# Linear attention and a SiLU feed-forward layer on one core: batch 1's exp(k), the PSUM banks of two chunks, a weight sum and the last store rearranged

## The chip, the core and the metric

The kernel runs on one NeuronCore of a Trainium2 chip. A core has a matrix engine (TensorE, PE, with its own path for loading weights, PEld), three engines for elementwise work (VectorE, DVE; ScalarE, ACT; GpSimd, POOL), a queue engine (SyncE, SP), and sixteen DMA engines that all the queues share. They run side by side and wait for each other by semaphores. TensorE writes its results to PSUM, here one tile of 8 banks of 512 float32 columns on 128 partitions. The metric is the device time of one execution in microseconds.

## What is computed

```python
def _attn_ref(q, k, v) -> np.ndarray:      # 8 batches, 8 heads, 576 rows, 64 columns
    q_s = q - np.max(q, axis=-1, keepdims=True)
    q_s = np.exp(q_s)
    q_s = q_s / (np.sum(q_s, axis=-1, keepdims=True) + 1e-09)
    k_s = k - np.max(k, axis=2, keepdims=True)
    k_s = np.exp(k_s)
    k_s = k_s / (np.sum(k_s, axis=2, keepdims=True) + 1e-09)
    kv = np.einsum('bhsd,bhse->bhde', k_s, v)
    return np.einsum('bhsd,bhde->bhse', q_s, kv).astype(np.float32)
...
def _moe_ref(x, w_in, w_out) -> np.ndarray:   # 4608 x 512, 512 x 2048, 2048 x 512
    h = x @ w_in
    g = h * (1.0 / (1.0 + np.exp(-h)))
    return (g @ w_out).astype(np.float32)
```

The attention's output, its heads side by side, is the `x` of the second function.

## The kernel before

**Batches and chunks.** A batch has 576 token rows. The feed-forward layer works on chunks of 512 token columns, nine in all, so that chunk 1 needs the end of batch 0 and most of batch 1. For each batch, ACT takes exp(q) and exp(k) (`exp_q` L105, `exp_k` L110), q is normalized on DVE or POOL (`qnorm` L152), v is cast into `vaug` (`vcast` L113), PE multiplies k and v (`kv` L183), DVE divides the result into `kvn` (`kvcopy` L195), and PE makes x from the transposed q and `kvn` (`xt` L236). Loads of q, k and v go through two buffers for each name and half, so a load of batch 2 waits until batch 1's reader of the same buffer has run.

**First stage.** Chunk 0 is computed with batch 0 whole (576 columns): sixteen `wide` units (L606) of the first product, each into two PSUM banks, followed by a tanh on ACT (L248) and one DVE pass (L249) that writes `GT`. Chunk 0's second product, `mm2_plain` (L394), accumulates into banks 2 to 5 over sixteen units. Chunk 1's first product, `mm1` (L288), is interleaved with its last six units; its sixteen products use the banks of the table `A1_BANKS` (L271), and each is followed by a tanh on ACT and a pass on DVE. When `mm2_plain` is done, `mm2_plain_out` (L404) takes two of its banks out, one by ACT (L408) and one by DVE (L410).

**Later chunks.** From chunk 2 on, both products use a Strassen-Winograd scheme with seven block products in place of eight. `group` (L345) is the first product: it uses banks 0 to 3, its adds are at L337 and its activations at L343. `prod` (L444) is the second product: by default it uses banks 4 and 5, with snapshots to SBUF by ACT (L474). Sums of weights that the scheme needs are made once: `ws_op` (L304) for the first weight matrix, `t_op` (L434) for the second; its second sum, T2 = B22 - T1, is made on DVE in two halves (L442), and its third and fourth on POOL. Sums of the data blocks are made by `s_op` (L423). The second product of the last chunk stands alone at the end and is written out in `end` (L725): the chain of products 1, 6 and 7 accumulates in bank 3, product 4 is in bank 1, 2 in bank 5, and 5 and 3 in banks 4 and 0. `part` (L703) makes a quarter of the output with one DVE instruction and stores it in two pieces, on the queues given there.

**Order.** The order is written out by hand. The work is a list of units; `plan(u, f)` (L603) puts a function ahead of unit u, in the order of the calls, and the loop at L801 runs all of it. Each engine executes its own instructions in that order. `b1` is 16, the first unit behind the wide stage. Unit b1 + 9 is the last `mm2_plain` unit without an interleaved `mm1`; from b1 + 10 to b1 + 21, `mm1` products 0 to 5 stand at even offsets and `mm2_plain` units at odd ones; `mm1` product 6 is unit b1 + 22, and so on to b1 + 31.

Of the kernel before, what the change touches and what calls it, by code (L numbers as in the profile page):

```python
# [17 lines left out]
def kernel(  # L18
# [9 lines left out]
    nc = tc.nc  # L28
# [64 lines left out]
    def load(b, name, src, cc, eng):  # L93
        t = ld.tile([128, 2, J * D], FP32, name=name)
        st[b][name, cc] = t
        x = src[b].rearrange("(g r) (p j) d -> g (r p) (j d)", r=2, j=J)
        eng.dma_start(out=t, in_=x.rearrange("g x y -> x g y")[:, 2 * cc:2 * cc + 2, :])  # L97

    def jgd(b, name, cc):
        return st[b][name, cc].rearrange("p g (j d) -> p j g d", d=D)  # L100

    def half(t, cc):
        return t[:, :, cc * 128:(cc + 1) * 128].rearrange("p j (g d) -> p j g d", d=D)

    def exp_q(b, cc):  # L105
        if "eq" not in st[b]:
            st[b]["eq"] = ap.tile([128, J, NG * D], BF16, name="eq")
        nc.scalar.activation(out=half(st[b]["eq"], cc), in_=jgd(b, "qt", cc), func=ACT.Exp)  # L108

    def exp_k(b, cc):  # L110
        nc.scalar.activation(out=half(ek, cc), in_=jgd(b, "kt", cc), func=ACT.Exp)  # L111
# [6 lines left out]
    def qsum_pair(b, cc):  # L118
        e = half(st[b]["eq"], cc)
        t1 = mp.tile([128, 2 * TCH], FP32, name="h0", bufs=1)[:, 0:J * D]  # L120
        t1 = t1.rearrange("p (j g d) -> p j g d", g=2, d=D // 2)
        t2 = mp.tile([128, 2 * TCH], FP32, name=f"h{cc + 1}", bufs=1)[:, 0:J * D // 2]
        t2 = t2.rearrange("p (j g d) -> p j g d", g=2, d=D // 4)
        nc.gpsimd.tensor_tensor(  # L124
            out=t1, in0=e[:, :, :, 0:D // 2], in1=e[:, :, :, D // 2:D], op=ALU.add
        )
        nc.gpsimd.tensor_tensor(
            out=t2, in0=t1[:, :, :, 0:D // 4], in1=t1[:, :, :, D // 4:D // 2], op=ALU.add
        )
        st[b]["t2", cc] = t2  # L130

    def qsum_end(b, cc):
        new_zq(b)
        nc.vector.reduce_sum(out=st[b]["zq"][:, cc], in_=st[b]["t2", cc], axis=AX.X)
        nc.vector.reciprocal(out=st[b]["rzq"][:, cc], in_=st[b]["zq"][:, cc])
# [16 lines left out]
    def qnorm(b, cc, eng):  # L152
        e = half(st[b]["eq"], cc)
        r = st[b]["rzq"][:, cc]
        eng.tensor_tensor(  # L155
            out=e, in0=e, in1=r[:, :, :, None].to_broadcast([128, J, 2, D]), op=ALU.mult
        )
# [110 lines left out]
            GTS[0][:, fb, :].rearrange("p (a n) -> p a n", a=2), S,  # L268
        )

    A1_BANKS = [0, 1, 0, 1, 0, 1, 2, 0, 3, 1, 0, 2, 1, 0, 2, 3]  # L271

    def mm1_mm(t, fb, bank, cs):
        o0 = pieces(t)[0][3]
        for c in cs:
            nc.tensor.matmul(  # L276
                out=PS[:, bank, o0:TCH],
                lhsT=W1[:, c, fb * 128:(fb + 1) * 128],
                rhs=XTS[t % 2][:, c, o0:TCH],
                start=(c == 0),  # L280
                stop=(c == NC - 1),
            )

    def mm1_silu(t, fb, bank):
        o0 = pieces(t)[0][3]
        silu(t, fb, PS[:, bank, o0:TCH], GTS[t % 2][:, fb, o0:TCH], TCH - o0)

    def mm1(t, i):  # L288
        mm1_mm(t, FB[i], A1_BANKS[i], range(NC))
        mm1_silu(t, FB[i], A1_BANKS[i])  # L290

# [94 lines left out]
    def rows(t, col):  # L386
        b, c = divmod(t * TCH + col, S)
        return out[b * S:(b + 1) * S, :].rearrange("(p j) o -> j p o", j=J)[c // P]
# [31 lines left out]
    def blk(t, kh, th):  # L420
        return GTS[t % 2][:, kh * HF:(kh + 1) * HF, th * HT:(th + 1) * HT]
# [12 lines left out]
    def t_op(i, eng, f0=0, f1=HF):  # L434
        o, in0, in1 = {
            1: (T1, B12, B11),
            2: (T2, B22, T1),
            3: (T3, B22, B12),
            4: (T4, B21, T2),
        }[i]  # L440
        f = slice(f0, f1)
        eng.tensor_tensor(out=o[:, f], in0=in0[:, f], in1=in1[:, f], op=ALU.subtract)  # L442

    def prod(t, i, m, bank=None, fresh=None, done=None):  # L444
        bank = WBANK[i] if bank is None else bank
        a, bb = {
            1: (blk(t, 0, 0), B11),
            2: (blk(t, 1, 0), B21),
            3: (SS[4], B22),
            4: (blk(t, 1, 1), T4),  # L450
            5: (SS[1], T1),
            6: (SS[2], T2),
            7: (blk(t, 0, 1), T3),
        }[i]
        first = (m == 0 and i in (1, 2, 5)) if fresh is None else fresh
        done = (m == 1 and i in (4, 3, 2)) if done is None else done
        for fc in range(HF):
            nc.tensor.matmul(  # L458
                out=PS[:, bank, m * HN:(m + 1) * HN],
                lhsT=a[:, fc, m * 128:(m + 1) * 128],  # L460
                rhs=bb[:, fc, :],
                start=(first and fc == 0),
                stop=(done and fc == HF - 1),
                skip_group_check=True,
            )

    def w_out_tile(t, m):
        if ("o", m) not in WG[t]:
            WG[t]["o", m] = mp.tile([128, 2, DM], FP32, name="ow", bufs=3)
        return WG[t]["o", m]  # L470

    def snap(t, name, bank=4):
        WG[t][name] = mp.tile([128, 512], FP32, name=name, bufs=1)
        nc.scalar.activation(out=WG[t][name], in_=PS[:, bank, :], func=ACT.Copy, scale=OS)  # L474
# [65 lines left out]
    def load_w2(f0, f1):  # L540
        nc.gpsimd.dma_start(
            out=W2[:, f0:f1, :],
            in_=w_out[f0 * 128:f1 * 128, :].rearrange("(fc p) o -> p fc o", p=128),
        )
# [58 lines left out]
    def plan(u, f):  # L603
        at.setdefault(u, []).append(f)
# [92 lines left out]
    last = NCH - 1  # L697
# [5 lines left out]
    def part(name, bank, th, n, a):  # L703
        o = w_out_tile(last, th)[:, a, n * HN:(n + 1) * HN]
        nc.vector.scalar_tensor_tensor(  # L705
            out=o,
            in0=PS[:, bank, a * HN:(a + 1) * HN],
            scalar=OS,
            in1=WG[last][name][:, a * HN:(a + 1) * HN],
            op0=ALU.mult,  # L710
            op1=ALU.add,
        )
        one, two = {
            (0, 0): (nc.sync, nc.sync),
            (1, 1): (nc.gpsimd, nc.gpsimd),
            (1, 0): (nc.scalar, nc.sync),
            (0, 1): (nc.scalar, nc.gpsimd) if a == 0 else (nc.sync, nc.sync),
        }[th, n]
        for i, eng in enumerate((one, two)):
            eng.dma_start(  # L720
                out=rows(last, th * HT + a * 128 + i * P)[:, n * HN:(n + 1) * HN],
                in_=o[i * P:(i + 1) * P, :],
            )

    def end(i, m):  # L725
        if i in (5, 3):
            prod(last, i, m, bank=(4, 0)[m], fresh=(i == 5), done=(i == 3))
        elif i == 4:
            prod(last, i, m, bank=1, fresh=(m == 0), done=(m == 1))
        else:  # L730
            prod(last, i, m, bank=5 if i == 2 else 3)
        if i == 3:
            part("sb", (4, 0)[m], 0, 1, m)
        elif m == 1 and i in (1, 6, 7):
            snap(last, {1: "sa", 6: "sb", 7: "sc"}[i], 3)
        if m == 1 and i == 2:
            part("sa", 5, 0, 0, 0)
            part("sa", 5, 0, 0, 1)
        elif m == 1 and i == 7:
            part("sc", 4, 1, 1, 0)  # L740
            part("sc", 0, 1, 1, 1)
        elif m == 1 and i == 4:
            part("sc", 1, 1, 0, 0)
            part("sc", 1, 1, 0, 1)

    for i in (1, 2, 6, 5, 7, 4, 3):
        for m in range(2):
# [3 lines left out]
    b1 = begin[1]  # L751
# [6 lines left out]
    plan(9, lambda: (load_w2(8, 12), exp_q(1, 0), qsum_pair(1, 0)))  # L758
    plan(10, lambda: (load(2, "qt", q, 0, nc.gpsimd), load(2, "qt", q, 1, nc.gpsimd)))
    plan(11, lambda: (exp_q(1, 1), qsum_end(1, 0), qnorm(1, 0, nc.gpsimd), qsum_pair(1, 1)))  # L760
    plan(13, lambda: exp_k(1, 0))
    plan(15, lambda: exp_k(1, 1))
    plan(b1, lambda: (tr(1, 0, 0, 5, 6), tr(1, 0, 5, J, 7)))
    plan(b1, lambda: (trcopy(1, 0, 0, 5, 6, nc.scalar), trcopy(1, 0, 5, J, 7)))
    plan(b1, lambda: (qsum_end(1, 1), qnorm(1, 1, nc.vector)))
    plan(b1, lambda: load_w2(12, 16))
    plan(b1, lambda: (load(2, "kt", k, 0, nc.gpsimd), load(2, "kt", k, 1, nc.gpsimd)))
    plan(b1, lambda: nc.gpsimd.tensor_copy(GTS[1][:, :, 0:64], GTS[0][:, :, TCH:S]))
    plan(b1 + 6, lambda: (load(2, "vt", v, 0, nc.gpsimd), load(2, "vt", v, 1, nc.gpsimd)))
    plan(b1 + 4, lambda: vcast(1, 0, nc.scalar))  # L770
    plan(b1 + 5, lambda: (tr(1, 1, 0, 5, 0), tr(1, 1, 5, J, 1)))
# [14 lines left out]
    plan(b1 + 14, lambda: q_transpose(2))  # L786
    for i, x in enumerate((16, 18)):
        plan(b1 + x, lambda i=i: (exp_k(2, i), vcast(2, i, nc.gpsimd)))
    plan(b1 + 18, lambda: t_op(2, nc.vector, 0, 4))
    plan(b1 + 20, lambda: t_op(2, nc.vector, 4, 8))  # L790
    plan(b1 + 20, lambda: loads(3, nc.sync))
    plan(b1 + 22, lambda: mm2_plain_out(0, (0, 1)))
    plan(b1 + 23, lambda: kv_both(2))
# [42 lines left out]
```

## Time and profile before

Device time over seven runs, and the one execution that was profiled:

| | us |
|---|---|
| median of 7 runs | 265.92 |
| lowest and highest | 264.84 to 266.93 |
| profiled execution, its time | 264.83 |
| its span, first to last instruction | 263.0 |
| from the span to the time, around it | 1.83 |
| PE busy | 254.8 |
| DVE busy | 209.7 |
| ACT busy | 182.6 |
| POOL busy | 74.7 |

The busy times are those of the profiled execution and overlap each other. A line of a timeline has the start in us, the length in us, the engine, the line of the kernel, the operation, what it writes and reads with partitions x elements, and how many instructions are merged in it; in brackets stands the idle time before it with what ended the wait. PE products are pipelined, so that the end of one is shown later than the start of the next. A line of a table by stage has the stretch, its length, then for PE, PEld, DVE, ACT and POOL the busy us with the number of instructions, and at the end the granted TensorE clock (1.00 is full), the mean share of the DMA engines in use, and GB/s.

### The profile page before, as it was taken

How to read it: one execution, taken by the hardware profiler on the slowest of the kernel's cores; microseconds unless marked ns; L12 is line 12 of the kernel's file. 1: busy time of each engine (PE TensorE's matmuls, PEld its weight loads, DVE VectorE, ACT ScalarE, POOL GpSimd, SP SyncE). 2: the span in 40 equal slices, each digit the busy share in tenths (PEclk: the TensorE clock that was granted, in tenths of full speed). 3: DMA queues.
4: the chain of work that ended last, by engine and by line, in shares of the span. 5: the costliest groups of instructions: out<-in, count | busy, mean ns of one | idle time of the engine just before them, and what ended most of it. 6: DMA issues, size and time to landing. Idle time of an engine off the chain costs nothing.

```text
span 263.0 us, 6375 instructions
## 1 busy us (share of the span) xinstructions
PE 254.8 (97%) x2708; PEld 201.4 (77%) x2708; DVE 209.7 (80%) x276; ACT 182.6 (69%) x209; POOL 74.7 (28%) x65
## 2 busy tenths in 40 slices
PE   8999999999999999999999999999999999999993
PEld 2467644445888888888888888888888888888782
DVE  2867789987997999799979997999798548855832
ACT  5767955748796699669966996699664747484610
POOL 1743981697360306030603060306000000000004
PEclk9999999999999999999999999999999999999999
DMA  7999999689978487957784878440415004300634
GB/s 244 331 200 330 259 324 333 242 168 384 331 267 195 130 210 260 171 154 193 275 199 129 209 260 206 121 107 2 90 36 126 2 0 92 70 2 1 134 68 120
DMA packets 35452, 45.89 MB, mean 174 GB/s; under 512 B 16208, under 2 KB 19984, under 8 KB 35424
## 3 DMA queue, kind: packets, MB, share of 16 engines
q1 hardware_dynamic: 29568, 33.69, 46.4%
q0 software_dynamic: 5616, 11.60, 16.8%
q8 instruction: 21, 0.34, 0.5%
q10 hardware_dynamic: 240, 0.20, 0.3%
q14 instruction: 7, 0.06, 0.1%
HBM read 36.70 MB, written 9.44 MB: 175 GB/s over the span
## 4 chain that ended last, share of the span: by engine, by line
PE 84%; DVE 6%; DMA 4%; ACT 2%; POOL 2%; SPq 1%; issue 1%; POOLq 0%; DVEq 0%; ACTq 0%
PE PS L458 36%; PE PS L359 33%; PE PS L256 4%; PE PS L276 4%; DMA vt<-in_v_dram 4%; PE PS L396 3%; PE PS L187 2%; PE PS L226 2%; DVE WS L312 1%; DVE GT L249 1%; DVE zq L148 1%; SPq L97 1%; POOL out_dram L720 1%; POOL h L124 0%; DVE h L337 0%
## 5 line engine op out<-in xcount | busy, mean ns | idle before, releaser
L337 DVE TENSOR_TENSOR h<-PS,h 128x1024 f32<-128x1024 f32 x42 | 50.7, 1207 | 11.2 <-PE PS L359 5.8
L458 PEld LDWEIGHTS <-GT 128*128 128x128 f16 x512 | 49.6, 98 | 7.4 <-issue 1.6
L458 PE MATMUL PS<-W,GT 128*128 128x256 f16 x384 | 49.1, 273 | 0.4 <-DVE h L337 0.4
L359 PEld LDWEIGHTS <-WS 128*128 128x128 f16 x448 | 43.7, 98 | 5.7 <-issue 0.6
L155 POOL TENSOR_TENSOR eq<-eq,rzq 128x1152 bf16<-128x1152 bf16 x13 | 27.5, 2117 | 60.3 <-DVE rzq L150 56.2
L359 PE MATMUL PS<-XS,WS 128*128 128x256 f16 x336 | 43.5, 273 | 0.0
L343 ACT ACTIVATE GT<-h 128x1024 f16<-128x1024 f32 x42 | 43.3, 1054 | 0.3 <-DVE h L337 0.3
L89 ACT COPY h<-PS 128x1024 f32<-128x1024 f32 x32 | 32.4, 1012 | 13.7 <-PE PS L359 13.3
L458 PEld LDWEIGHTS <-S 128*128 128x128 f16 x384 | 37.2, 98 | 5.2 <-issue 1.0
L359 PEld LDWEIGHTS <-W 128*128 128x128 f16 x336 | 32.5, 98 | 4.4 <-issue 0.2
L458 PE MATMUL PS<-T,S 128*128 128x256 f16 x256 | 32.7, 273 | 0.0
L359 PE MATMUL PS<-XT,W 128*128 128x256 f16 x224 | 27.9, 273 | 0.0
L249 DVE SCALAR_TENSOR_TENSOR GT<-sg,PS 128x576 f16<-128x576 f32 (+1 forms) x32 | 21.2, 680 | 8.2 <-ACT sg L248 8.0
L343 ACT ACTIVATE GT<-PS 128x1024 f16<-128x1024 f32 x14 | 14.3, 1023 | 19.1 <-PE PS L359 19.0
L248 ACT ACTIVATE sg<-PS 128x576 f32<-128x576 f32 (+1 forms) x32 | 18.8, 598 | 9.5 <-PE PS L276 5.4
L91 POOL CAST vaug<-vt 128x1152 bf16<-128x1152 f32 x12 | 15.0, 1259 | 34.2 <-DMA vt<-in_v_dram 33.8
L720 POOL DMA_DIRECT2D out_dram<-ow x5 | 2.7, 546 | 72.7 <-DVE ow L705 72.7
L108 ACT ACTIVATE eq<-qt 128x1152 bf16<-128x1152 f32 x16 | 18.6, 1165 | 2.5 <-DMA qt<-in_q_dram 2.5
L111 ACT ACTIVATE ek<-kt 128x1152 bf16<-128x1152 f32 x16 | 18.5, 1153 | 1.4 <-DMA kt<-in_k_dram 1.4
L146 DVE TENSOR_REDUCE zq<-eq 128x18 f32<-128x1152 bf16 x12 | 16.1, 1344 | 3.7 <-ACT eq L108 3.7
L256 PE MATMUL PS<-XT,W 128*128 128x288 f16 x128 | 16.5, 286 | 0.7 <-DVE GT L249 0.4
L458 PE MATMUL PS<-W,S 128*128 128x256 f16 x128 | 16.5, 273 | 0.0
(78 smaller groups left out, 349.9 us busy)
## 6 DMA issues: line engine op xcount, KB each, us to landing
out_dram<-ow SPq DMA_DIRECT2D x64, 128.0 KB, 2.4
qt<-in_q_dram SPq DMA_DIRECT2D x12, 576.0 KB, 4.8
kt<-in_k_dram SPq DMA_DIRECT2D x12, 576.0 KB, 6.1
vt<-in_v_dram SPq DMA_DIRECT2D x12, 576.0 KB, 5.3
qt<-in_q_dram POOLq DMA_DIRECT2D x4, 576.0 KB, 13.5
kt<-in_k_dram POOLq DMA_DIRECT2D x4, 576.0 KB, 13.7
vt<-in_v_dram POOLq DMA_DIRECT2D x4, 576.0 KB, 12.9
W<-in_moe_w_out_dram POOLq DMA_DIRECT2D x4, 512.0 KB, 15.3
```

Of the source, the lines that this page charges most:

```text
L89: eng.copy(out=o, in_=i)
L108: nc.scalar.activation(out=half(st[b]["eq"], cc), in_=jgd(b, "qt", cc), func=ACT.Exp)
L111: nc.scalar.activation(out=half(ek, cc), in_=jgd(b, "kt", cc), func=ACT.Exp)
L146: nc.vector.reduce_sum(out=z, in_=e, axis=AX.X)
L155: eng.tensor_tensor(out=e, in0=e, in1=r[:, :, :, None].to_broadcast([128, J, 2, D]), op=ALU.mult)
L248: nc.scalar.activation(out=s, in_=i, func=ACT.Tanh, scale=OS)
L249: nc.vector.scalar_tensor_tensor(out=o, in0=s, scalar=1.0, in1=i, op0=ALU.add, op1=ALU.mult)
L256: nc.tensor.matmul(out=PS[:, 2 * (fb % 3) + n, 0:S // 2], lhsT=W1[:, c, fb * 128:(fb + 1) * 128], rhs=XTS[0][:, c, n * (S // 2):(n + 1) * ...
L337: nc.vector.tensor_tensor(out=H[i], in0=PS[:, 2:4, :].rearrange("p b n -> p (b n)"), in1=H[i], op=ALU.add)
L343: nc.scalar.activation(out=group_out(t, f, n), in_=x, func=ACT.Silu, scale=1.0 / XS)
L359: nc.tensor.matmul(out=PS[:, bank + p // 2, (p % 2) * HT:(p % 2 + 1) * HT], lhsT=a[:, c, p * 128:(p + 1) * 128], rhs=bb[:, c, :], start=(i ...
L458: nc.tensor.matmul(out=PS[:, bank, m * HN:(m + 1) * HN], lhsT=a[:, fc, m * 128:(m + 1) * 128], rhs=bb[:, fc, :], start=(first and fc == 0) ...
```

## The change

There are four edits.

1. `exp_k(1, 0)` and `exp_k(1, 1)` move from ahead of units 13 and 15 (the wide stage) to ahead of units b1 + 1 and b1 + 2. The two loads of batch 2's k move from b1 to b1 + 3, and so behind POOL's copy into `GTS[1]`.
2. In `A1_BANKS`, products 6, 7, 8 and 9 get banks 0, 2, 1, 3 instead of 2, 0, 3, 1. The two halves of `t_op(2)` move two units later, so that each stands behind the pass of one more `mm1` product: products 4 and 5.
3. In `end`, the chain of products 1, 6 and 7 is in bank 1 and product 4 in bank 3.
4. The last quarter's second piece is stored from the ACT queue instead of SP's.

On PE and SP, the order of the instructions stays as it is, but for the store that goes from SP to ACT; on ACT, DVE and POOL the moved instructions change places as described.

```diff
-    A1_BANKS = [0, 1, 0, 1, 0, 1, 2, 0, 3, 1, 0, 2, 1, 0, 2, 3]
+    A1_BANKS = [0, 1, 0, 1, 0, 1, 0, 2, 1, 3, 0, 2, 1, 0, 2, 3]
...
-            (0, 1): (nc.scalar, nc.gpsimd) if a == 0 else (nc.sync, nc.sync),
+            (0, 1): (nc.scalar, nc.gpsimd) if a == 0 else (nc.sync, nc.scalar),
...
         elif i == 4:
-            prod(last, i, m, bank=1, fresh=(m == 0), done=(m == 1))
+            prod(last, i, m, bank=3, fresh=(m == 0), done=(m == 1))
         else:
-            prod(last, i, m, bank=5 if i == 2 else 3)
+            prod(last, i, m, bank=5 if i == 2 else 1)
         if i == 3:
             part("sb", (4, 0)[m], 0, 1, m)
         elif m == 1 and i in (1, 6, 7):
-            snap(last, {1: "sa", 6: "sb", 7: "sc"}[i], 3)
+            snap(last, {1: "sa", 6: "sb", 7: "sc"}[i], 1)
...
-            part("sc", 1, 1, 0, 0)
-            part("sc", 1, 1, 0, 1)
+            part("sc", 3, 1, 0, 0)
+            part("sc", 3, 1, 0, 1)
...
-    plan(13, lambda: exp_k(1, 0))
-    plan(15, lambda: exp_k(1, 1))
+    plan(b1 + 1, lambda: exp_k(1, 0))
+    plan(b1 + 2, lambda: exp_k(1, 1))
...
-    plan(b1, lambda: (load(2, "kt", k, 0, nc.gpsimd), load(2, "kt", k, 1, nc.gpsimd)))
     plan(b1, lambda: nc.gpsimd.tensor_copy(GTS[1][:, :, 0:64], GTS[0][:, :, TCH:S]))
+    plan(b1 + 3, lambda: (load(2, "kt", k, 0, nc.gpsimd), load(2, "kt", k, 1, nc.gpsimd)))
...
-    plan(b1 + 18, lambda: t_op(2, nc.vector, 0, 4))
-    plan(b1 + 20, lambda: t_op(2, nc.vector, 4, 8))
+    plan(b1 + 20, lambda: t_op(2, nc.vector, 0, 4))
+    plan(b1 + 22, lambda: t_op(2, nc.vector, 4, 8))
```

## The prediction

> **What bounds the kernel now.** I read the page's head first, then the busy time by stage, then who TensorE (PE) waited for, then the orders of VectorE (DVE), ScalarE (ACT) and GpSimd (POOL) around each wait.
>
> ```profile
> span 263.0 us, 6375 instructions
> PE 254.8 (97%) x2708; PEld 201.4 (77%) x2708; DVE 209.7 (80%) x276; ACT 182.6 (69%) x209; POOL 74.7 (28%) x65
> ...
> 66.00:245.00 179.00, 178.94 (x1998) 155.19 (x1996) 150.58 (x177) 133.77 (x143) 33.05 (x20) 1.00 0.53 141
> 245.00:263.00 18.00, 13.16 (x120) 11.39 (x117) 8.44 (x14) 3.76 (x5) 2.70 (x5) 1.00 0.51 118
> ```
>
> PE is busy 254.8 of 263.0 us at the full granted clock, and from 66 to 245 us it misses 0.06 us. No edit removes PE work, so only PE's waits before 66 us, one wait near 246 us, and what follows the last product can change. The view of waits lists what PE waited for (total, times, longest):
>
> ```profile
> PE PS L458 <- DVE h L337: 0.4, 1, 0.4
> PE PS L256 <- DVE GT L249: 0.4, 2, 0.2
> PE PS L276 <- DVE GT L249: 0.3, 1, 0.3
> PE PS L276 <- ACT ow L408: 0.3, 1, 0.3
> ```
>
> These understate the loss: a 256-column product is shown 0.273 us long but follows the one before after 0.109. By starts, the L458 wait is 0.61 us (245.501 to 246.217, less 0.109) and the ACT ow wait 0.42 (53.989 to 54.624, less a 512-column step of 0.216).
>
> **Part 1: batch 1's exp(k).** Two ACT instructions (L111, 29.64 and 31.96, 1.16 us each) leave the wide stage. No PE wait goes with them: PE's gap at 27.92 ends before the first of them; that at 30.23 ends with DVE's GT, which stood behind the q sum that POOL delivers; and the transposes at 32.38 wait for POOL's eq (30.20 + 2.13 = 32.33). In the new place they run at about 33.5 to 35.8, behind the qT copy. ACT now idles 2.36 us there until vt lands (36.60), just room for 2 x 1.16, and PE first reads ek at 39.53. Cost and gain: 0.
>
> The two kt loads that reuse these buffers go behind POOL's L768 copy: issue at 36.3 and 37.0 instead of 35.17 and 35.88. The queue's backlog hides that: pieces issued at 34.38, 35.17, 35.88, 38.05 and 40.21 landed at 45.90, 47.36, 48.86, 50.34 and 51.80, one per 1.5 us whatever their issue. Were the cover gone, they would land 1.1 us later, at 48.5 and 50.0; exp(k) of batch 2 reads them at 48.52 and 50.27, still 0. The vt loads behind them wait for ACT's casts (38.05, 40.21) as before.
>
> The copy L768 itself moves from 36.60 to 35.17. There DVE is to start the second q normalization (L155; 35.47 now, 35.26 once GT's last piece is earlier, bound by POOL's q sum ending 34.44 plus 0.45 and 0.27). **Here a rule speaks against the change**: the Trainium skill, SBUF — State Buffer, section "SBUF: two separate sides", says that DVE (with two SBUF inputs) and GpSimd share a port pair that the first starter holds for its whole instruction. The rows agree, shown by what moved next to this copy:
>
> ```profile
> 36.60 1.12 POOL L768 COPY GT<-GT 128x1024 f16<-128x1024 f16 x1
> ...
> 36.74 1.52 DVE L312 TENSOR_TENSOR WS<-W 128x1024 f16<-128x1024 f16 x1
> 38.30 0.69 DVE L312 TENSOR_TENSOR WS<-WS,W 128x1024 f16<-128x1024 f16 x1
> ```
>
> The weight sum that starts 0.14 behind the copy ends 0.55 after the copy's end; alone it takes 0.69. By the row's 1.36 us, free of conflict, the normalization ends at 36.6 and PE's transposes (37.21) don't wait. By the rule it ends 36.29 + 1.22 = 37.51 (1.36 less the 0.14 that goes on beforehand) and PE loses 0.33. The start order is decided by 0.09 us, so ends 0 and +0.33; I take +0.17, a race on which no row is closer than 0.14.
>
> **Part 2: banks of products 6 to 9, and W2's second sum.** Product 6 goes into bank 0, so it waits for product 4's DVE pass (L249) instead of ACT's output of bank 2 (L408). For this the two halves of the sum L442 go behind the passes of products 4 and 5.
>
> ```profile
> 50.35 1.09 DVE L249 SCALAR_TENSOR_TENSOR GT<-sg,PS 128x448 f16<-128x448 f32 x2
> 51.36 1.91 DVE L442 TENSOR_TENSOR T<-W,T 128x1024 f16<-128x1024 f16 x1
> 53.19 0.61 DVE L249 SCALAR_TENSOR_TENSOR GT<-sg,PS 128x448 f16<-128x448 f32 x1
> 53.72 1.10 DVE L442 TENSOR_TENSOR T<-W,T 128x1024 f16<-128x1024 f16 x1
> ...
> 48.52 4.19 POOL L155 TENSOR_TENSOR eq<-eq,rzq 128x1152 bf16<-128x1152 bf16 x2 [7.60 <-DVE rzq L150]
> 52.67 3.17 POOL L91 CAST vaug<-vt 128x1152 bf16<-128x1152 f32 x2
> ```
>
> Product 4's tanh ends on ACT at 52.47, so its pass runs 52.50 to 53.11 (DVE idle from 51.44) and product 6 starts at 54.20 instead of 54.62. Gain 0.42, but next on PE stand batch 2's k·v products. Their second half waits for POOL's second cast (52.67 + 3.17 = 55.84; PE at 55.89). If that cast stays, the whole 0.42 is lost again.
>
> The same port says that it doesn't stay. The casts take 1.61 and 1.62 us here, 1.16 elsewhere (L91 on POOL, from 68 us on). The first stood behind the sum that had waited for POOL's normalization, the second behind the sum's other half. By their own durations the moved halves would run 53.02 to 54.93 and so on; by the lock, first half: starts 53.02 under the cast running from 52.67, goes on when that ends, unhindered, at 53.83, ends 54.37; second cast 53.78 + 1.62 = 55.40; pass of product 5 to 54.91; second half 54.82, waits until 55.40, ends 55.94. k·v's second half then starts at 55.44, 0.45 earlier.
>
> What is late next is DVE: the bank 3 output to 56.54, product 6's pass to 57.08, then reciprocal and two products of kvn (0.17, and 0.49 together) to 57.70. The x product (L226, 57.93 now, 57.46 by PE's own order) waits for them and for the transposed q, landed at 57.58: start 57.74. **Part 2 brings 0.19**, bounds -0.5 (casts unhindered, nothing late) and +1.2 (below). GpSimd's third and fourth sums start 0.17 later (55.97), with 2.7 us of idle time behind them. Products 8, 9, 10, 12 and 15 find their banks free over 0.5 us ahead.
>
> **Part 3: last chunk's chain in bank 1.** The first product of the last chain (L458, 246.22) waited for DVE's add of banks 2 and 3 (L337, 244.94 + 1.23). Bank 1 was last read by ACT's activation ending 244.02. PE goes on at 245.61: gain 0.61. Next stands product 2's weight load behind ACT's L343, which needs that same add (246.20 to 247.26): PE comes at 247.36 instead of 247.97, about 0.04 too early. The rest has room: S2 at 248.09 for 249.1, the snapshot to 248.2, bank 5 free since 246.76. **Gain 0.57**, bounds 0.4 and 0.61. Bank 3 for product 4 was read long before (246.17 for 254.3).
>
> **Part 4: last store.** Both pieces went by SP, issued at 259.09 and 259.61, landing 261.60 and 261.92. Now ACT issues the second, free at 259.41, so at about 259.47. The Trainium skill (DMA: Bandwidth & Descriptors, "Issuing engines are not separate DMA queues") has this save the sequencer's issue time alone: 0.14 earlier. The rows: ACT's three stores here land 2.75, 3.26 and 2.58 us after their issue, SP's last 2.31. With 2.58 it lands at 262.05, +0.13. I take the rows: **+0.13**, bounds -0.15 and +0.8 (the 3.26 row).
>
> **Sum** on the profiled execution (264.83 us; span 263.0 and 1.83 around it): 0 + 0.17 - 0.19 - 0.57 + 0.13 = -0.46. The median of the seven runs, 265.92, stands 1.09 above that execution; the same -0.46 gives about 265.4.
>
> **Rivals.**
> - *More comes through.* DVE wins the port ahead of the copy (0), the x product waits only for the transposed q (57.63, gain 0.30), the store saves 0.15: -0.57 - 0.30 - 0.15 = -1.0, 264.9. For it: each is within 0.15 us of being decided so. Against: all three at once.
> - *It doesn't do what it says in the middle.* The casts still end at 55.84 and the copy takes the port: +0.33 - 0.57 + 0.13 = -0.1, 265.8. For it: POOL is in one unbroken run from 48.5 to 63.9. Against: the cast's 1.16 elsewhere.
> - *Slower: W2's sums hold kvn.* If each moved half takes the 1.91 us of its present first row, they end at 54.93 and 57.29, kvn at 59.05, the x product starts at 59.1 instead of 57.93: +1.16, with +0.17 - 0.57 + 0.13 about +0.9, 266.8. It decides from where kvn comes later than 58.2, 0.5 us behind my forecast. Against: that 1.91 contains 1.36 us beside POOL's normalization, over by then.
>
> **How the numbers follow.** Forecast 0.42, more 0.37, not in the middle 0.10, slower 0.11. A measurement of this kernel tells about 0.3%, 0.8 us, from no change. Of the forecast case (-0.2 to -0.9) I put 0.10 past 0.8 us: faster 0.10 + 0.37 = 0.47; same 0.32 + 0.10 = 0.42; slower 0.11. Range: from 264.5 (the "more" case less 0.4 for the runs' own spread) to 266.2 (the middle case plus 0.4); the slower case lies outside.
>
> **What would show it.** Right: no L458 wait on L337, and the last chain starting 0.6 us after the add's start; no L276 wait on ow; POOL's first cast at 1.16 and the second at 1.6 us; L442's halves near 1.35 and 1.1; kvn ending near 57.7 and an L226 wait on it. Wrong: a PE wait at the transposes near 37.2 (copy first) or none; casts still ending past 55.8; kvn past 58.2; a last landing more than 3.5 us behind PE's last product. The whole is wrong if the stretch from 66 to 245 us gets longer.

## The result, and the profile after

The changed kernel takes 267.46 us (median of 26 runs, 266.46 to 268.34) against 265.93 for the kernel before (61 runs on the same chip, 264.84 to 267.32). The ratio is 1.0052, 95% interval 1.0042 to 1.0062: slower by 1.4 us or so, where 0.5 us faster was forecast. The profiled execution took 266.82 us with a span of 265.0; against before's 264.83 and 263.0 that is 2.0 us more, since before's profiled run happens to lie 1.1 us under its median and this one 0.6.

The work is the same: the head of the page has PE at 254.9 us as before. What grew is PE's waiting.

```profile
span 265.0 us, 6377 instructions
PE 254.9 (96%) x2708; PEld 201.2 (76%) x2708; DVE 209.8 (79%) x276; ACT 183.0 (69%) x209; POOL 74.0 (28%) x65
...
q8 instruction: 21, 0.34, 0.5%
```

(The last line, from the page's table of DMA queues, has packets, MB and share; it is used below.) The view of PE's waits (total us, times, longest) names what is new:

```profile
PE PS L226 <- DMA qT<-eq: 1.5, 2, 1.2
...
PE PS L173 <- DVE eq L155: 0.5, 1, 0.5
...
PE PS L359 <- DVE XS L321: 0.2, 1, 0.2
PE PS L226 <- DVE kvn L200: 0.2, 1, 0.2
```

Of before's lines, L458 on L337 and L276 on ow are gone, as meant. In their place stand the x product's wait for the transposed q, and three smaller ones. The transposed q is batch 2's normalized exp(q), which a DMA transposes (L165). PE's timeline shows where PE waits; first after, then before:

```profile
54.58 0.92 PE L276 MATMUL PS<-XT,W 128*128 128x448 f16 x4
55.43 0.86 PE L187 MATMUL PS<-vaug,ek 64*64 64x65 bf16 x72
56.22 1.69 PE L276 MATMUL PS<-XT,W 128*128 128x448 f16 x8
58.09 0.25 PE L226 MATMUL PS<-qT,kvn 64*64 64x128 bf16 x4 [0.18 <-DVE kvn L200]
59.57 0.36 PE L226 MATMUL PS<-qT,kvn 64*64 64x384 bf16 x4 [1.23 <-DMA qT<-eq]
```

```profile
54.62 0.92 PE L276 MATMUL PS<-XT,W 128*128 128x448 f16 x4 [0.26 <-ACT ow L408]
55.47 0.91 PE L187 MATMUL PS<-vaug,ek 64*64 64x65 bf16 x72
56.31 1.69 PE L276 MATMUL PS<-XT,W 128*128 128x448 f16 x8
57.93 0.25 PE L226 MATMUL PS<-qT,kvn 64*64 64x128 bf16 x4
```

The first four x products of batch 2 use rows that are there; the second four use the last rows of the transposed q. Before, they follow without a gap (58.01); after, they wait until 59.57. Reading both traces at the start of the same product gives the account, after less before, running total in us:

| same product in both | before at | shift | what it went by |
|---|---|---|---|
| first stage | 15.5 | +0.08 | ahead of any edit |
| batch 1's second half transposed (L173) | 37.2 | +0.36 | DVE's normalization ends 37.52 |
| `mm1` product 6 (L276) | 54.6 | -0.04 | wait on ow gone: -0.40 |
| x product of batch 2, first four (L226) | 57.9 | +0.16 | kvn |
| x product, second four | 58.0 | +1.56 | **transposed q: +1.40** |
| chunk 2's first product with XS (L359) | 66.9 | +2.00 | DVE's XS sums: +0.44 |
| chunk 3's first product (L359) | 108.6 | +2.27 | small waits ahead: +0.27 |
| second product behind chunk 3's x (L458) | 118.7 | +2.66 | chunk 3's transposed q: +0.39 |
| last chain in bank 1 (L458) | 246.2 | +2.05 | part 3: -0.60 |
| last store landed | 261.9 | +1.95 | end: -0.10 |

The transposed q comes late for a reason that no engine's row shows. The view of its line, after and before, has the two numbers that matter: where the first of six starts, and at the end the longest time from issue to landing.

```profile
L165 SPq DMA_TRANSPOSE qT<-eq x6: 2767/2794/2989, 53.1 to 186.5; - x6
...
DMA to landing us min/median/max: 4.6/5.1/6.4
```

```profile
L165 SPq DMA_TRANSPOSE qT<-eq x6: 2737/2780/2889, 52.7 to 183.8; - x6
...
DMA to landing us min/median/max: 4.6/4.8/5.9
```

The transposition for batch 2 is the first of the six. It is issued at 53.12 instead of 52.74, because POOL's normalization, like all the work there, runs 0.36 later; and it lands 6.41 us after its issue instead of 4.84: 59.53, and PE starts 0.04 behind. So 0.38 of the delay is a later issue and 1.57 a longer transfer. The maximum in before's line, 5.9, is chunk 3's: the kernel before has one long transfer already. After, that one takes 6.25.

The wait at 66.9 is a second result of this. DVE's first XS sum (L321) and POOL's cast of batch 3 now fall together. DVE's timeline after, then POOL's after, then DVE's before:

```profile
67.08 1.34 DVE L321 TENSOR_TENSOR XS<-XT 128x512 f16<-128x512 f16 x1
68.45 0.42 DVE L321 TENSOR_TENSOR XS<-XT,XS 128x512 f16<-128x512 f16 x1
```

```profile
66.98 1.16 POOL L91 CAST vaug<-vt 128x1152 bf16<-128x1152 f32 x1 [2.52 <-DMA vt<-in_v_dram]
```

```profile
65.49 0.42 DVE L321 TENSOR_TENSOR XS<-XT 128x512 f16<-128x512 f16 x1
```

The cast starts when its load has landed, which PE's delay doesn't move. Before, DVE was 1.1 us ahead of it. Now the sum starts 0.1 us behind the cast and takes 1.34 us in place of 0.42.

### The profile page after: what moved, and what is told of

It is laid out like the page before. It is cut to its first block, busy times and chain, and to the rows that moved or that the text cites. A ratio compares the mean times of both kernels' runs of the same rounds, so it can differ in the third digit from the quotient of the medians.

```text
span 265.0 us, 6377 instructions
## 1 busy us (share of the span) xinstructions
PE 254.9 (96%) x2708; PEld 201.2 (76%) x2708; DVE 209.8 (79%) x276; ACT 183.0 (69%) x209; POOL 74.0 (28%) x65
## 4 chain that ended last, share of the span: by engine, by line
PE 64%; DVE 16%; DMA 8%; POOL 5%; ACT 2%; issue 2%; SPq 1%; POOLq 0%; DVEq 0%; ACTq 0%
PE PS L458 30%; PE PS L359 26%; DMA qT<-eq 5%; DMA vt<-in_v_dram 4%; PE PS L256 3%; POOL eq L155 3%; DVE h L337 2%; DVE zq L146 2%; DVE GT L249 2%; DVE S L432 2%; PE PS L226 2%; DVE WS L312 1%; PE PS L187 1%; POOL h L124 1%; DVE h L91 1%
## 5 line engine op out<-in xcount | busy, mean ns | idle before, releaser
L337 DVE TENSOR_TENSOR h<-PS,h 128x1024 f32<-128x1024 f32 x42 | 50.7, 1207 | 11.6 <-PE PS L359 6.2
L458 PEld LDWEIGHTS <-GT 128*128 128x128 f16 x512 | 49.6, 98 | 6.9 <-issue 1.0
L458 PE MATMUL PS<-W,GT 128*128 128x256 f16 x384 | 49.1, 273 | 0.0
L359 PEld LDWEIGHTS <-WS 128*128 128x128 f16 x448 | 43.6, 98 | 6.3 <-issue 0.7
L359 PE MATMUL PS<-XS,WS 128*128 128x256 f16 x336 | 43.5, 273 | 0.4 <-DVE XS L321 0.2
L458 PEld LDWEIGHTS <-S 128*128 128x128 f16 x384 | 37.1, 98 | 5.4 <-issue 1.0
L359 PEld LDWEIGHTS <-W 128*128 128x128 f16 x336 | 32.5, 98 | 4.4 <-issue 0.2
L458 PE MATMUL PS<-T,S 128*128 128x256 f16 x256 | 32.7, 273 | 0.0
L359 PE MATMUL PS<-XT,W 128*128 128x256 f16 x224 | 27.9, 273 | 0.0
L91 POOL CAST vaug<-vt 128x1152 bf16<-128x1152 f32 x12 | 14.4, 1206 | 35.1 <-DMA vt<-in_v_dram 34.8
L146 DVE TENSOR_REDUCE zq<-eq 128x18 f32<-128x1152 bf16 x12 | 16.2, 1346 | 3.8 <-ACT eq L108 3.8
L458 PE MATMUL PS<-W,S 128*128 128x256 f16 x128 | 16.5, 273 | 0.0
```

The lines of the kernel that those rows point to most:

```text
L146: nc.vector.reduce_sum(out=z, in_=e, axis=AX.X)
L337: nc.vector.tensor_tensor(out=H[i], in0=PS[:, 2:4, :].rearrange("p b n -> p (b n)"), in1=H[i], op=ALU.add)
L359: nc.tensor.matmul(out=PS[:, bank + p // 2, (p % 2) * HT:(p % 2 + 1) * HT], lhsT=a[:, c, p * 128:(p + 1) * 128], rhs=bb[:, c, :], start=(i ...
L458: nc.tensor.matmul(out=PS[:, bank, m * HN:(m + 1) * HN], lhsT=a[:, fc, m * 128:(m + 1) * 128], rhs=bb[:, fc, :], start=(first and fc == 0) ...
```

## Experiments

All ratios are against the kernel before, run on the same chip in the same series, with 95% intervals. Where a kernel has extra or fewer warming products, these write to PSUM banks whose content nothing uses, so the output isn't changed by them.

### Each part by itself

First series (kernel before: 266.0 us): part 1 alone, part 2 alone, part 3 alone, and all four parts with the x products of batch 2 two units later, so that PE has other work while a late transposed q is on its way. The first three are the diff's own hunks for exp(k), kt loads and copy; for `A1_BANKS` and `t_op`; for `end`'s banks. The fourth is as below. In these tables the time is a median, and the last column is from the one profiled execution of each kernel.

```diff
-    for i, x in enumerate((25, 28)):
+    for i, x in enumerate((27, 30)):
         plan(b1 + x, lambda i=i: xt(2, i))
```

> Part 1 alone (exp(k), the k loads, POOL's copy). Fetch theory: PE waits 0.3 us at the transposes near 37.3 (POOL's copy holds the port while DVE normalizes q), and the DMA transpose of batch 2's q and PE both move back by that 0.3. The transpose lands 4.8 us after its issue if the last engine's completion packet goes ahead of PE's 16 KB instruction fetch near 57.4, and 6.4 if it goes behind it: +0.3 or +1.7 us, and the trace shows which order it was. Rival 'issue time' (a transpose issued after 53.1 runs into the loads queued behind it and always lands late): lands 6.4 us after its issue, +1.7. Rival 'banks and W2' (the loss comes from part 2): +0.3 at most, landing 4.8.

> Part 2 alone (banks of products 6 to 9, W2's second sum two units later). Fetch theory: the transpose is issued at 52.74 as before, but PE stands 0.4 us further when k.v is done, so it asks for its next 16 KB of instructions earlier; that fetch gets ahead of the last completion packet, the transposed q lands near 59 instead of 57.6, and the kernel is 1 to 1.4 us slower. Rival 'issue time': issued at 52.74, it lands at 57.6, and the part gains 0.2 to 0.3. Rival 'banks and W2': slower by over 1 us with the transpose landing at 57.6, PE waiting for kvn or for a bank.

> Part 3 alone (last chain in bank 1). All theories: nothing before 245 us changes, the L458 wait on DVE's L337 goes, -0.57 us.

> All four parts, and batch 2's x products (both halves) two products of chunk 1 later, so that PE works on while the transposed q is on its way. Fetch theory: the 1.5 us wait of L226 on the DMA goes (two products are 1.5 us), and the kernel is 1.2 to 1.5 us faster than with the four parts alone, about -0.1 to -0.5 against before. Rival 'banks and W2' or anything that holds PE elsewhere: the wait moves to another place and the time stays at +1.5.

| kernel | us | ratio | transposed q lands after its issue |
|---|---|---|---|
| part 1 alone | 265.93 | 0.9998 [0.9984, 1.0012] | 4.69 us |
| part 2 alone | 268.96 | 1.0101 [1.0072, 1.0130] | 6.41 us |
| part 3 alone | 265.64 | 0.9983 [0.9970, 0.9997] | 4.85 us |
| all four, x products later | 265.19 | 0.9966 [0.9949, 0.9984] | 6.54 us |

**Part 2 alone makes the kernel slow**, by more than all four together. Its PE timeline has the same hole:

```profile
54.63 0.92 PE L276 MATMUL PS<-XT,W 128*128 128x448 f16 x4
55.48 0.86 PE L187 MATMUL PS<-vaug,ek 64*64 64x65 bf16 x72
...
59.62 0.36 PE L226 MATMUL PS<-qT,kvn 64*64 64x384 bf16 x4 [1.23 <-DMA qT<-eq]
```

Chunk 2's second and fourth XS sums then lie on POOL's two casts of batch 3 (1.26 and 1.37 us in place of 0.42), and PE waits a further 1.0 us behind them. And with the x products two units later, all four parts make the lowest ratio of the study, though its interval overlaps that of part 3 alone: the transposition is as slow as ever (6.54), but PE finds eight more products of `mm1` ahead of it and waits 0.2 us:

```profile
56.61 3.20 PE L276 MATMUL PS<-XT,W 128*128 128x448 f16 x16
59.74 0.69 PE L226 MATMUL PS<-qT,kvn 64*64 64x128 bf16 x8
```

**Part 1 makes no difference that the medians can tell** (0.9998; the interval ends at +0.3 us). In before's profile DVE's normalization takes 1.36 us; behind POOL's copy it takes 2.17 or 2.18, in all six profiles that have part 1. Of after:

```profile
35.24 1.05 POOL L767 COPY GT<-GT 128x1024 f16<-128x1024 f16 x1
...
35.34 2.18 DVE L155 TENSOR_TENSOR eq<-eq,rzq 128x1152 bf16<-128x1152 bf16 x1
```

But the order of before has no fixed time either. Beside the same two load issues on POOL it takes 1.36 us once more (part 3 with later x products, in the next series), 1.75 in two profiles, 1.88 and 1.91 in those of parts 2 and 3, and 2.15 in two. What makes it differ isn't shown. Part 3's profile, whose first stage is that of before, has +0.33 there against before's, and +0.47 at chunk 3's transposed q. So the 0.36 and 0.39 of the account lie within what kernels without parts 1 and 2 show, and needn't be the change's doing. That the medians are 1.5 us apart and not the 2.0 of the profiles fits this.

Part 3 does what was meant: the last chain no longer waits. After, then before:

```profile
248.27 1.91 PE L458 MATMUL PS<-W,GT 128*128 128x256 f16 x16
```

```profile
246.22 3.65 PE L458 MATMUL PS<-W,GT 128*128 128x256 f16 x32 [0.44 <-DVE h L337]
```

### What makes the transposition late

Packets in the trace's DMA records give the lead. A transposition ends with 32 packets of 4 bytes, two for each of 16 DMA engines if they are shared out evenly. After, thirty of them come by 4.20 us after the issue, as in before, and the last two at 5.35 and 5.36 (4.33 in before). Fifteen of the sixteen reports of the landing are in by 4.86 us, and the last comes at 6.41. Meanwhile one packet of 16 KB on queue 8 runs from 4.40 to 5.36; in before it starts at 4.34, behind all 32. That queue is the one on the page called instruction: 21 packets of 0.34 MB in all, 16 KB each, for PE's 2 x 2708 instructions, one packet for each 256. The Trainium skill, Runtime: NRT & Kernel Launch, section "Instruction fetch mechanics", has the same size: an engine refills its instructions in blocks of 16 KiB, 256 at a time, by a DMA queue of its own, and the cost of crossing a block boundary is "mostly hidden". The number agrees, and no wait of PE in before's profile goes with it. But from a transfer that is under way, it seems, the fetch is not hidden.

So one theory: PE asks for its next block when it reaches a certain instruction, and this request falls into the transposition. Part 2 lets PE be 0.4 us earlier against the transposition, and that is enough. One rival: traffic (the loads of batch 3 on SP) or POOL's port makes it late, and the count of PE's instructions doesn't matter. A second rival is PE's place in its work: that PE comes earlier might matter by itself. The test is to move the request without moving the work. The kernel warms PE with products of no use at the start (`heat`); with more of them the same work has higher instruction numbers, and each block is asked for earlier in it.

Second series (kernel before: 266.28 us). All four parts with eight warming products fewer; **the kernel before with three more**; and two kernels without part 2:

```diff
     # the kernel before, request earlier
-    heat(7)
+    heat(9)
...
-    heat(3, 6)
+    heat(4, 6)
```

> All four parts, with 8 of the warming products at the start left out (they write nothing that is used): PE's instruction stream is 16 instructions shorter ahead of the fetch near 57.5 us, so that block is asked for some 1.5 us later in PE's work, after the transposed q has landed. Fetch theory: all 16 engines report within 4.9 us of the transpose's issue, PE's wait of 1.5 us for it goes, and the kernel is 1.2 to 1.9 us faster than with the four parts (265.6 to 266.3). Rival 'PE comes too early' (PE's earlier arrival alone makes the wait, whatever is fetched): the transpose lands after 6.4 us as before and the time stays near 267.4.

> The kernel before, none of the four parts, with 3 warming products more at the start (6 PE instructions): the fetch near 57 us is asked for 0.5 to 0.6 us earlier in PE's work, as it is with part 2. Fetch theory: the transposed q lands about 6.4 us after its issue instead of 4.8, PE waits about 1 us for it, and the kernel is 1 to 2 us slower although no bank, sum or exp(k) was touched. Rival 'PE comes too early': PE's place in the program is unchanged, the transpose lands after 4.8 us; at most +0.2 us for the three products.

> Part 3 (last chain in bank 1) and batch 2's x products two products later, without parts 1, 2 and 4. It tells what parts 1 and 2 bring once the wait for the transposed q is covered: fetch theory says about 0.3 us (their 0.42 at product 6 less DVE's later kvn), so this is near -0.5 us against before and 0.2 to 0.4 above all four parts with the x products later. If parts 1 and 2 are themselves harmful, this is faster than that one.

> Parts 3 and 4 alone. The store from ACT's queue is expected at -0.15 to +0.15 us beside part 3 alone (265.64): the last landing 2.3 to 2.6 us after its issue.

| kernel | us | ratio | transposed q lands after its issue |
|---|---|---|---|
| all four, 8 warming products fewer | 267.94 | 1.0080 [1.0050, 1.0111] | 6.38 us |
| before, 3 warming products more | 268.65 | 1.0103 [1.0080, 1.0125] | 6.54 us |
| part 3, x products later | 266.04 | 1.0005 [0.9986, 1.0025] | 4.67 us |
| parts 3 and 4 | 265.44 | 0.9973 [0.9959, 0.9986] | 4.65 us |

The second row is the strongest of the study. It has none of the four edits, and although all of it runs 1.07 us later than in before's profile by then, product 6 starts as far behind the transposition's issue as there (1.89 and 1.88 us). The 1.07 us aren't the reason: the profile of parts 3 and 4 (last row) runs 1.00 us late at the same place, and its transposed q lands in time. Six PE instructions more, and the kernel before has the changed kernel's hole, while the old wait on ow is still there:

```profile
55.70 0.92 PE L276 MATMUL PS<-XT,W 128*128 128x448 f16 x4 [0.26 <-ACT ow L408]
...
60.40 0.36 PE L226 MATMUL PS<-qT,kvn 64*64 64x384 bf16 x4 [1.14 <-DMA qT<-eq]
```

The first row is a miss. Sixteen PE instructions fewer didn't get the request out of the way: where the boundary lies PE does batch 2's k·v products, which start 0.01 us apart, so that the request moved by some 0.06 us in relation to the transposition. The fewer warming products cost 1.3 us besides, between 15 and 20 us, where the row of granted clocks has a 7 in its third slice:

```profile
PEclk9979999999999999999999999999999999999998
```

The third row is a miss too: with nothing to cover, the later x products bring nothing and seem to take back part 3's gain (0.17%), though the intervals overlap. All four parts with the later x products are 0.4% lower (0.9966, in the first series), with intervals that just don't touch: with the wait covered, the other parts do seem to bring something. Part 4 beside part 3 is within the intervals of part 3 alone.

The third series (kernel before: 265.91 us) moves the block boundaries by far more: 88 products of 8 columns, worth little time, come in place of two warming ones, 172 PE instructions more in all. All four parts with them; the kernel before with them as the control; parts 3 and 4 with them. And, without them, parts 1, 3 and 4:

```diff
+    def tiny(n, bank):
+        for i in range(n):
+            r, s = (i // 2) % 2, i % 2
+            nc.tensor.matmul(
+                out=PS[s * 64:(s + 1) * 64, bank + r, 0:8],
+                lhsT=warm[r * 64:(r + 1) * 64, 0:64],
+                rhs=warm[r * 64:(r + 1) * 64, 0:8],
...
-    heat(7)
+    heat(6)
+    tiny(50, 4)
...
-    heat(3, 6)
+    heat(2, 6)
+    tiny(38, 6)
```

> All four parts; at the start two warming products are replaced by 88 very small ones (8 columns, into banks that nobody reads), so that PE's instruction stream is 172 instructions longer ahead of the fetch: that block is now asked for near PE's work of 53 us, before the transposed q's data move at 54.4. This shift is ten times that of the run that left 8 products out, whose fetch still began 4.4 us after the transpose's issue. Fetch theory: no fetch in the last us of batch 2's transpose, all 16 engines report within 4.9 us, PE's wait for it goes (0.3 at most stays, for kvn), and the kernel is 1.2 to 1.9 us faster than the four parts alone, less up to 0.8 us for the small products. Rival 'PE comes too early': landing 6.4 us after issue, time 267.4 or more.

> The kernel before with the same small products: the control. Both theories: batch 2's transpose lands after 4.7 to 4.9 us, and the time is 0 to +0.8 us against before for the small products (less if chunk 3's transpose, at present 5.9 to 6.2 us, is freed as well).

> Parts 3 and 4 with the same small products: beside all four parts with them it tells what parts 1 and 2 bring when no fetch meets the transpose. Fetch theory: all four are 0 to 0.3 us faster than this. It should be 0.7 us below the control.

> Parts 1, 3 and 4, without part 2. Fetch theory: PE stands where it stood relative to the transpose (its product 4.3 us after the issue, not 3.9), the transpose lands after 4.7 to 4.9 us, and the kernel is 0.5 to 0.8 us faster than before: part 2 alone makes the change slow. If it is slow all the same (+1 us or more), part 1 or the store has a share.

| kernel | us | ratio | transposed q lands after its issue |
|---|---|---|---|
| all four, 172 PE instructions more | 268.42 | 1.0088 [1.0067, 1.0108] | 4.67 us |
| before, 172 more (the control) | 270.38 | 1.0158 [1.0127, 1.0190] | 4.64 us |
| parts 3 and 4, 172 more | 269.53 | 1.0135 [1.0104, 1.0166] | 4.66 us |
| parts 1, 3 and 4, nothing else | 265.34 | 0.9984 [0.9973, 0.9995] | 4.67 us |

With all four parts and the boundaries elsewhere, the hole is closed; the x products follow kvn, in one group:

```profile
59.96 1.69 PE L276 MATMUL PS<-XT,W 128*128 128x448 f16 x8
61.83 0.41 PE L226 MATMUL PS<-qT,kvn 64*64 64x128 bf16 x8 [0.18 <-DVE kvn L200]
```

This is not a transposition without a fetch. The request that was meant is far away (its packet comes at 47.8 us, 9 us ahead of the issue), but the next block is now asked for in the same k·v products, 0.4 us later than in the changed kernel; its packet runs from 4.22 to 5.17 us after the issue and holds nothing up.

The totals miss what was expected (0 to +0.8 us for the control, +4.5 measured), since the small products have a price of their own at the start. PE stands for 2.55 us with no wait that the profile shows, and one block of 16 KB is fetched meanwhile (15.3 to 16.2 us), so that it seems to have run out of instructions; in two of the three profiles it then goes on at a lower clock for a while.

```profile
14.78 0.44 PE L226 MATMUL PS<-qT,kvn 64*64 64x320 bf16 x7
17.77 0.27 PE L226 MATMUL PS<-qT,kvn 64*64 64x256 bf16 x1 [2.55 <-issue]
```

The stall is 2.6, 3.0 and 2.1 us in the three profiles, and the three kernels' runs spread over 267.0 to 271.4 us. So the totals say little, and the traces more, from 20 us to the last product. There, against before's profile, all four parts go from +3.80 to +3.69 us, where the changed kernel goes from +0.08 to +2.06. The control goes from +5.23 to +6.57, and parts 3 and 4 from +2.25 to +2.19: all four parts are now ahead of the control by 1.4 us, but not of parts 3 and 4. The last row confirms the start: without part 2 the other three are faster than before, by 0.05 to 0.27%.

### What the runs say together

| profiled kernel | PE at its 915th row, after the issue | last two small packets | landing |
|---|---|---|---|
| before, 3 warming products more | 2.08 us | 5.43 us | 6.54 us |
| part 2 alone; all four; all four, later x; all four, 8 fewer | 2.32 to 2.38 | 5.34 to 5.42 | 6.38 to 6.54 |
| before; parts 1; 3; 3 and 4; 1, 3 and 4; 3 and later x | 2.73 | 4.19 to 4.33 | 4.65 to 4.85 |

A row is a product or a weight load in the trace; the 915th belongs to batch 2's first k·v products, or to product 6 in the first line. It was chosen afterwards: any number from 912 to 918 parts the eleven kernels without the small products without an exception. With these the next boundary, 256 rows on, comes by at 2.75 to 3.21 us, and the transposition isn't held up. In all five late profiles the last small packet starts within 0.005 us of the end of the 16 KB packet.

Two kernels separate PE's place from its count of instructions. Before with 3 warming products more has product 6 where before has it (1.89 us after the issue), and the transposition is late; all four with 172 instructions more has it where the changed kernel has it (1.46), and it isn't.

The other transpositions of these traces agree in part. There are 84, six in each of 14 profiles. The 18 that take 5.87 to 6.54 us, chunk 3's in the kernel before among them, all have a fetch packet that starts 3.3 to 4.5 us after the issue, and in the four kernels whose boundaries were moved most (8 warming products fewer, and those with the small products) chunk 3's lands after 4.59 to 4.63. But 19 others have such a packet too and take 5.0 us or less, and the fourth transposition takes 5.5 to 5.8 us in all 14 profiles although no fetch starts then. So a fetch is not the only thing that can delay one.

**Shown** is that the number of PE's instructions ahead decides whether batch 2's transposition is late, that the late ones end with a fetch of instructions, and that this wait, with what follows from it, is the loss. **Not shown** is what happens within the DMA engine: the records don't name it. The Trainium skill, DMA: Bandwidth & Descriptors, section "Queues, rings and completion order", has each engine take turns between its queues by whole packets; that would fit a wait behind a packet that has begun. But with part 1 alone, with parts 1, 3 and 4, and with part 3 and later x products the fetch starts 0.01 to 0.12 us ahead of the last small packets and doesn't hold them. Why a boundary that PE passes 2.1 to 2.4 us after the issue does harm, and one at 2.7 doesn't, stays open too; the request itself isn't recorded.

## Why the prediction was wrong, point by point

- **The step that failed is in part 2: the x product "waits for them and for the transposed q, landed at 57.58: start 57.74".** The landing was taken over from before as a fixed time. The transfer took 6.41 us instead of 4.84 because of the edit's own gain, and the second half of the product started at 59.57. The bounds of part 2 reached to +1.2 only by way of kvn; the mechanism had no place in any rival. It cost 1.40 us at once, and 0.44 at the XS sums behind it. "The whole is wrong if the stretch from 66 to 245 us gets longer" was an alarm on the right side: from 68 to 247 us PE misses 0.73 us where it missed 0.06. Most of the loss lies ahead of that stretch, though, and of the 0.73 chunk 3's transposed q takes 0.31, which parts 1 and 3 alone wait for too.
- **The rest of part 2 was right.** Product 6 came 0.40 earlier (0.42 forecast). The casts fell as the lock has it: first 1.14, second 1.62, ended at 55.76. Less the 0.36 by which all of this runs later, that is 55.40, the forecast. The halves of T2 took 1.32 and 1.10 (1.35 and 1.1). kvn ended at 58.04, less 0.36 57.68 (57.70), and the first four x products do wait for it:

```profile
53.04 2.71 POOL L91 CAST vaug<-vt 128x1152 bf16<-128x1152 f32 x2
...
53.41 1.32 DVE L442 TENSOR_TENSOR T<-W,T 128x1024 f16<-128x1024 f16 x1
...
57.55 0.49 DVE L200 TENSOR_TENSOR kvn<-PS,rz 128x128 bf16<-128x128 f32 x2
```

- **Part 1: +0.17 was taken, between 0 and 0.33.** In the profile POOL's copy won the port (35.24, DVE 35.34, end 37.52; 37.51 forecast), +0.33 by the rule. The rule was right: 2.17 or 2.18 us in all six profiles with part 1. The row that it was weighed against isn't fixed (1.36 to 2.15 us with the order of before), and the medians show no cost, though +0.17 would lie within their interval.
- **Part 3: -0.57 forecast, -0.60 in the trace;** alone 265.64 against 266.0 us.
- **Part 4: +0.13 forecast, -0.10 in the trace.** ACT's store landed 2.30 us after its issue where the row of 2.58 was taken. Too small for the medians to tell.
- **Rivals.** "More comes through" (-1.0) couldn't come, since it wants the x product to start with the transposed q at 57.63. The rival "in the middle" (-0.1) had the casts still end at 55.84, and they ended 0.4 earlier, as said. "Slower" had the sign and came nearest (266.8) by chance, with the wrong cause: kvn held back four x products by 0.2 us and no more, and the halves of T2 took what was forecast.

## What to carry to other kernels

A transfer's time to landing is not a constant of the transfer: when an edit moves one engine against a DMA that it later waits for, ask what else comes on the DMA queues at that point, the engine's own instruction blocks among them (one of 16 KB for each 256 instructions here), and give a wait that has no slack some cover before a gain is put ahead of it. Here two numbers in a plan, the x products two units later, turned a loss of 0.5% into a gain of 0.2 to 0.5%. And a change of a few harmless instructions can move such a boundary, so a kernel without slack is to be compared with a control that has the same instruction count.

## What the runs showed of the hardware beyond that

- A fetch of 16 KB of PE's instructions took 0.88 to 2.06 us as one packet in these traces. In five profiles the last two of a transposition's 32 small packets came at its end, 1.0 to 1.2 us later than in the others, and the landing was 1.5 to 1.9 us later.
- With 88 products of 8 columns at the start, PE stood 2.1 to 3.0 us without a wait that the profile shows; that it had run out of instructions is inferred.
- A two-input sum on DVE beside two DMA issues on POOL (L97, 1.43 us for both) took anything from 1.36 to 2.15 us in eight profiles; the reason is open.
